# First queries and keys in two loads of 288 tokens, first scores in two steps, other offsets in the opening stretch

## The chip, the cores and the metric

One core of one Trainium2 chip. The metric is the device time of one execution in microseconds (us). The kernel before took 434.92 us, the median of 3 runs (434.41 to 435.18). Its program orders every instruction when it is built; nothing of the order is decided on the chip.

## The reference

Three stages, for 4 batches of 576 tokens, all in float32.

Stage 1 is attention with 8 heads of 64 values. Heads 0 to 3 look at the last 32 tokens (local), heads 4 to 7 at every 32nd token back (strided):

```python
mask_local = (rel >= 0) & (rel < stride)
mask_strided = (rel >= 0) & (pos[None, :] % stride == pos[:, None] % stride)
...
scores = np.where(masks[None, :, :, :], scores, -1000000000.0)
...
attn = attn / (np.sum(attn, axis=-1, keepdims=True) + 1e-09)
return np.matmul(attn, v).astype(np.float32)
```

Stage 2 is a gated block: `relu(x @ w_in)` is halved into u and v, v is normalised over its 512 features, mixed over the tokens with `w_spatial`, multiplied by u and projected by `w_out`. Stage 3 is four causal attention experts of width 64, of which each token takes the best two.

## The kernel before, in words

Every stage is written as small generators of steps. A step names its engine (or a choice of engines), a cost, what it needs and which buffers it takes. `Plan.run` (line 413 in the file, in class `Plan` from line 343) plays the steps through on a model of the five engines and emits them in that order: of the steps that can start first on an engine, the one with the lowest rank goes. The rank is given where a step is added (lines 1641 to 1724) plus an offset from the table NUDGE; HOLD delays a step's first start, and LEAN tilts the choice of engine. So three tables of numbers set the order of the work, on SP's queue of transfers too.

Attention works on pairs of heads: batch b, pair hp (0 and 1 local, 2 and 3 strided). `a1_load` (line 788) loads 64 + 64 rows of queries (line 796) and of keys (line 799), each a tile of 128 partitions by 576 tokens, 288 KB. `a1_load_v` (line 806) loads the values (line 818). `a1_scores` (line 826) does the small score matmuls (local: 36 blocks of 32 queries by 64 keys in two passes each, line 844; strided: line 856) in one step, into two PSUM tiles, one for each group of query blocks. `a1_local` (line 860) and `a1_strided` (line 916) mask a group on VectorE (lines 870 and 932), take the exponential on ScalarE (lines 879, 899) and scale by the sums, mostly on GpSimd (line 914). `a1_turn` transposes the weights on TensorE (lines 981, 983), and `a1_values` multiplies with the values (line 1050) and splits the result into a high and a low part, xh and xl (xl on VectorE, line 1062).

`weight` (line 652) loads a block of 128 rows of a weight (`w_in`: 512 KB of float64 bits, line 666, three buffers) and unpacks it, mostly on VectorE (lines 673 to 689 for the first half of the columns, the blocks W00 to W03; lines 673 to 698 and three matmuls at lines 705 to 707 for the second half, W10 to W13). Dense products are three matmuls for each pair of blocks (lines 618 to 620). `v_half` needs x of batch 0 and W10 to W13, block by block; `u_half` needs W00 to W03 as well. Until 46 us on its model, the planner fills TensorE's gaps with matmuls on zeros (`fill`, line 531), which compute nothing.

The ranks at the start: `a1_load` of batch 0 has 1.6 hp, `a1_load_v` 1.6 hp + 2.2, W1k 0.1 + 1.6 k, W0k 5 + k, and the attention of batch 1 has 100 + hp; to each comes its offset.

Of the kernel before, what the change touches and what calls it, by code (L numbers as in the profile page):

```python
# [1783 lines left out]
```

## Time and profile before

| what | value |
|---|---|
| median of 3 runs | 434.92 us (434.41 to 435.18) |
| the profiled execution | 434.02 us, of which the span of the profile is 432.1 us |
| TensorE, VectorE, ScalarE, GpSimd busy | 419.5, 318.7, 267.1, 141.1 us |
| data moved | 43.58 MB, mean 101 GB/s |
| granted TensorE clock | 0.998 over the span |

The profile shows one execution. The span runs from the first instruction to the last; 1.9 us lie around it. Busy times of different engines overlap. A row of the timeline gives start, busy time, engine, line, operation, tiles, count and, in brackets, how long the engine had been idle and for whom.

### The profile page before, as it was taken

To read this page: it belongs to the slowest core of one execution; us is meant where nothing else is said; L and a number is where in the kernel's file an instruction comes from. 1 tells how busy PE (TensorE), PEld (TensorE's weight loads), DVE (VectorE), ACT (ScalarE), POOL (GpSimd) and SP (SyncE) were. 2 spreads that over 40 slices of the span, in tenths; PEclk is the share of its full clock that TensorE was granted. 3 is DMA by queue.
4 is the path that set the end of the run, shared out by engine and by line. 5 is a ranking of instruction groups with operands and counts; after the bars stand their busy time and mean duration, and the time that the engine had idled before them with its cause. 6 is when DMAs were issued, how large, how long until landed. Compare 5 with 4: busy or idle time off the path is not lost.

```text
span 432.1 us, 11509 instructions
## 1 busy us (share of the span) xinstructions
PE 419.5 (97%) x4156; PEld 382.7 (89%) x4156; DVE 318.7 (74%) x1189; ACT 267.1 (62%) x827; POOL 141.1 (33%) x258
## 2 busy tenths in 40 slices
PE   7869999999999999999999999999999999999996
PEld 3557899999999889998999899999999999988885
DVE  6998998264577742347979863698888899988872
ACT  3666776154598841224405532887788779779973
POOL 3551876541152340221508911112022005215210
PEclk9999999999999999999999999999999999999999
DMA  7999105121561000334000006805251332162043
GB/s 297 340 361 308 35 2 175 67 79 36 157 205 44 2 2 2 122 101 167 2 1 2 2 0 155 194 1 126 67 134 43 94 79 58 24 160 98 26 148 121
DMA packets 22844, 43.58 MB, mean 101 GB/s; under 512 B 3202, under 2 KB 5634, under 8 KB 22788
## 3 DMA queue, kind: packets, MB, share of 16 engines
q1 hardware_dynamic: 22628, 42.72, 32.9%
q8 instruction: 33, 0.54, 0.5%
q14 instruction: 23, 0.19, 0.1%
q10 hardware_dynamic: 160, 0.13, 0.1%
HBM read 26.59 MB, written 4.72 MB: 72 GB/s over the span
## 4 chain that ended last, share of the span: by engine, by line
PE 95%; DVE 1%; DMA 1%; issue 1%; ACT 1%; POOL 0%; SPq 0%; ACTq 0%
PE pd L618 17%; PE pd L620 17%; PE pd L619 17%; PE pt L1488 4%; PE pd L1206 4%; PE pd L1207 4%; PE pd L1208 4%; PE px L1050 4%; PE ps L856 2%; PE px L1536 2%; PE ps L1401 2%; PE ps L1400 2%; PE px L1534 2%; PE px L1566 2%; PE pt L981 2%; PE pd L1210 1%
## 5 line engine op out<-in xcount | busy, mean ns | idle before, releaser
L1423 POOL TENSOR_SCALAR a<-a,asums 128x256 f32<-128x256 f32 (+3 forms) x23 | 23.1, 1010 | 87.1 <-DVE asums L1431 52.5
L914 POOL TENSOR_TENSOR a<-a,rs 128x216 f32<-128x216 f32 (+5 forms) x32 | 25.3, 797 | 55.2 <-DVE rs L912 26.3
L618 PE MATMUL pd<-xh,wh 128*128 128x288 f32 x128 | 38.8, 303 | 0.0
L1388 DVE CUSTOM_DVE_ANT_0 a<-ps,mqk 128x512 f32<-128x512 f32 (+4 forms) x72 | 33.5, 482 | 7.2 <-PE ps L1401 5.3
L1414 ACT ACTIVATE a<-a,amx 128x384 f32<-128x384 f32 (+3 forms) x64 | 35.6, 557 | 5.0 <-DVE amx L1388 4.9
L1206 PE MATMUL pd<-wh,vh 128*128 128x288 f32 x128 | 38.2, 298 | 0.0
L618 PE MATMUL pd<-gh,fh 128*128 128x288 f32 x128 | 38.1, 297 | 0.0
L619 PE MATMUL pd<-xl,wh 128*128 128x288 f32 x128 | 37.7, 295 | 0.0
L620 PE MATMUL pd<-gh,fl 128*128 128x288 f32 x128 | 37.7, 295 | 0.0
L1207 PE MATMUL pd<-wl,vh 128*128 128x288 f32 x128 | 37.7, 294 | 0.0
L620 PE MATMUL pd<-xh,wl 128*128 128x288 f32 x128 | 37.7, 294 | 0.0
L619 PE MATMUL pd<-gl,fh 128*128 128x288 f32 x128 | 37.7, 294 | 0.0
L1208 PE MATMUL pd<-wh,vlo 128*128 128x288 f32 x128 | 37.7, 294 | 0.0
L1121 DVE BATCH_NORM_STATS2 bst<-vr 128x6 f32<-128x512 f32 x18 | 12.4, 691 | 25.2 <-ACT vr L645 25.2
L1477 DVE TENSOR_TENSOR e<-pt,e 128x384 fp32r<-128x384 f32 (+1 forms) x48 | 27.6, 598 | 3.7 <-ACT e L639 3.2
L645 ACT ACTIVATE vr<-pd 128x512 f32<-128x512 f32 x17 | 10.1, 594 | 30.5 <-PE pd L620 29.0
L1214 DVE TENSOR_TENSOR u<-pd,u 128x288 f32<-128x288 f32 x32 | 13.9, 454 | 18.7 <-PE pd L1211 18.6
L1127 POOL TENSOR_TENSOR rstd<-rstd,neghalf 128x1 f32<-128x1 f32 x18 | 11.9, 664 | 47.4 <-DVE rstd L1125 38.7
L879 ACT ACTIVATE a<-a,mx 128x64 f32<-128x64 f32 (+1 forms) x72 | 24.9, 350 | 3.5 <-DVE mx L870 3.5
L618 PE MATMUL pd<-wh,xh 128*128 128x512 f32 x64 | 26.0, 406 | 0.0
L620 PE MATMUL pd<-wh,xl 128*128 128x512 f32 x64 | 25.1, 392 | 0.0
L619 PE MATMUL pd<-wl,xh 128*128 128x512 f32 x64 | 25.1, 392 | 0.0
(243 smaller groups left out, 1478.3 us busy)
## 6 DMA issues: line engine op xcount, KB each, us to landing
qk<-qk SPq DMA_DIRECT2D x64, 144.0 KB, 2.4
q<-in_qk_dram SPq DMA_DIRECT2D x16, 288.0 KB, 5.2
k<-in_qk_dram SPq DMA_DIRECT2D x16, 288.0 KB, 5.3
w<-in_win_dram SPq DMA_DIRECT2D x8, 512.0 KB, 6.3
out_dram<-o SPq DMA_DIRECT2D x16, 256.0 KB, 2.1
v<-in_vl_dram SPq DMA_DIRECT2D x8, 256.0 KB, 5.9
v<-in_vs_dram SPq DMA_DIRECT2D x8, 256.0 KB, 4.4
w<-in_woutT_dram SPq DMA_DIRECT2D x4, 512.0 KB, 4.4
```

The lines of the kernel that those rows point to most:

```text
L618: pe.matmul(ps, ah, bh, start=i == 0, stop=False)
L619: pe.matmul(ps, ah, bl, start=False, stop=False)
L620: pe.matmul(ps, al, bh, start=False, stop=i == n - 1)
L879: act.activation(a[:, c], a[:, c], AF.Exp, bias=mx[:, c:c + 1], scale=-1.0, accum_out=sums[:, c, :1])
L914: engine().tensor_mul(x, x, rs[:, :n].unsqueeze(2).broadcast_to([128, n, nk]))
L1206: pe.matmul(ps, vh[:, fs], wh[:, c0:c0 + cn], start=(i == 0), stop=False)
L1207: pe.matmul(ps, vh[:, fs], wl[:, c0:c0 + cn], start=False, stop=False)
L1208: pe.matmul(ps, vlo[:, fs], wh[:, c0:c0 + cn], start=False, stop=False)
L1388: dve.tensor_tensor_reduce(a[:, s0:s0 + sn], ps, mask, op0=ALU.add, op1=ALU.min, scale=-0.125, scalar=m if s0 else 3.0e38, accum_out=m)
L1414: act.activation(a, a, AF.Exp, bias=m, scale=-1.0, accum_out=st["sums", e][:, i:i + 1])
L1423: engine().tensor_scalar_mul(a, a, r)
L1477: dve.tensor_sub(el, ps, f(eh))
```

## The change

`a1_load` of the first pair of batch 0 loads queries and keys together, 288 tokens at a time, in two transfers; all other pairs load as before. `a1_scores` of that pair becomes two steps, one for each group, the first of which needs only the first transfer; a block of scores whose keys lie on both sides of token 288 becomes two matmuls. The event that the masks wait for is now one for each group. And the three tables are changed for the opening: the attention of batches 0 to 2, the `w_in` and spatial weights, and the first blocks of the dense products. The code, and of the tables the lines that set the first loads:

```diff
@@ NUDGE
-    'a1_load 0 0': -5.25, 'a1_load 0 1': -1.96, 'a1_load 0 2': 1.29, 'a1_load 0 3': 1, 'a1_load 1 0': 23.44,
...
+    'a1_load 0 0': -1.11, 'a1_load 0 2': 1.3, 'a1_load 0 3': 58.8, 'a1_load 1 0': -381.96, 'a1_load 1 1': 1.22,
+    'a1_load 1 2': -2.35, 'a1_load 1 3': -69.44, 'a1_load 2 0': 25.77, 'a1_load 2 1': -135.56, 'a1_load 2 2': 2.11,
+    'a1_load 3 1': 80.57, 'a1_load 3 2': 28.5, 'a1_load 3 3': 78.2, 'a1_load_v 0 0': 6.27, 'a1_load_v 0 1': 8.2,
+    'a1_load_v 0 2': 71.35, 'a1_load_v 0 3': 69.82, 'a1_load_v 1 0': 2.52, 'a1_load_v 1 1': -2.32,
...
-    'values 1 0': -15.65, 'values 1 1': -15.65, 'values 1 2': -15.61, 'values 1 3': -15.65, 'values 2 0': 0.85,
-    'values 2 1': -0.49, 'values 2 4': -8.96, "weight [('in', 0, 0)]": -10.61, "weight [('in', 0, 1)]": -0.46,
-    "weight [('in', 0, 2)]": -3.43, "weight [('in', 0, 3)]": -0.42, "weight [('in', 1, 0)]": -0.75,
-    "weight [('in', 1, 1)]": 1.68, "weight [('in', 1, 3)]": 0.53, "weight [('outT', 0)]": -4.4,
...
+    'values 1 3': -15.65, 'values 2 0': 0.85, 'values 2 1': -0.49, 'values 2 4': -8.96, "weight [('in', 0, 0)]": 0.06,
+    "weight [('in', 0, 2)]": -4.14, "weight [('in', 0, 3)]": -0.44, "weight [('in', 1, 1)]": 2.61,
+    "weight [('in', 1, 2)]": 0.1, "weight [('in', 1, 3)]": -0.23, "weight [('outT', 0)]": -4.4,
...
@@ HOLD
-    'a1_load 0 1': 2.27, 'a1_load 0 3': 0.02, 'a1_load 1 0': 0.9, 'a1_load 1 3': 1.52, 'a1_load 2 0': 20.87,
...
+    'a1_load 1 0': 0.5, 'a1_load 1 1': 0.03, 'a1_load 1 3': 3.52, 'a1_load 2 0': 20.03, 'a1_load 2 1': 7.79,
...
+    'values 3 0': 8.99, "weight [('in', 0, 0)]": 6.38, "weight [('in', 0, 2)]": 0.16, "weight [('in', 0, 3)]": 1.87,
+    "weight [('in', 1, 1)]": 2.04, "weight [('in', 1, 3)]": 7.88, "weight [('outT', 1)]": 0.58,
...
@@ a1_load
-        qt, kt = C([128, S], F, "q"), C([128, S], F, "k")
-        nc.sync.dma_start(qt, qk[b, hp, :, 0, :])
...
+        if n:
+            qt, kt = C([128, S], F, "q"), C([128, S], F, "k")
...
+        else:
+            qt, kt = [], []
+            for i, (c0, cn) in enumerate(HALVES):
+                if i:
+                    yield "sp", 0.46, (), {}
+                t = C([128, 2, cn], F, "qk1")
+                nc.sync.dma_start(t, qk[b, hp, :, :, c0:c0 + cn])
+                plan.dma(128 * 2 * cn * 4)
+                plan.set(("qk", b, hp, i), plan.ready - plan.end)
+                qt.append(t[:, 0])
+                kt.append(t[:, 1])
...
@@ a1_scores
-        yield "pe", (0.8 if large else 1.15 if local else 0.95), [("qk", b, hp)], dict(s=2)
...
+        def product(out, r, q0, qn, k0, kn):
+            if type(qt) is not list:
+                pe.matmul(out, qt[r, q0:q0 + qn], kt[r, k0:k0 + kn], start=True, stop=True)
+                return
+            q = qt[q0 // 288][r, q0 % 288:q0 % 288 + qn]
+            cut = min(max(288 - k0, 0), kn)
+            for c0, c1 in ((0, cut), (cut, kn)):
+                if c0 < c1:
+                    i = (k0 + c0) // 288
+                    pe.matmul(out[:, c0:c1], q, kt[i][r, k0 + c0 - 288 * i:k0 + c1 - 288 * i], start=True, stop=True)
+
+        whole_pair = b or hp
+        cost = 0.8 if large else 1.15 if local else 0.95
+        for groups in ((0, 1),) if whole_pair else ((0,), (1,)):
+            yield ("pe", cost if whole_pair else cost / 2, [("qk", b, hp) if whole_pair else ("qk", b, hp, groups[0])],
+                   dict(s=len(groups)))
...
+            if groups == (0,):
+                plan.set(("s1", b, hp, 0))
...
@@ a1_local
-        yield "dve", t_dve(n * nk, n), [("mask", "wide" if wide(b, hp) else True), ("s1", b, hp)], dict(c=1, mx=1)
+        yield "dve", t_dve(n * nk, n), [("mask", "wide" if wide(b, hp) else True), ("s1", b, hp, g)], dict(c=1, mx=1)
```

## Rows read from the trace of the kernel before

**Rows 1.** The page: busy time of each engine, and the chain by engine

```profile
PE 419.5 (97%) x4156; PEld 382.7 (89%) x4156; DVE 318.7 (74%) x1189; ACT 267.1 (62%) x827; POOL 141.1 (33%) x258
...
PE 95%; DVE 1%; DMA 1%; issue 1%; ACT 1%; POOL 0%; SPq 0%; ACTq 0%
```

**Rows 2.** Busy time by stretch: length, engines, then clock, DMA share, GB/s

```profile
0.00:5.04 5.04, 3.59 (x8) 1.04 (x8) 1.32 (x7) 1.49 (x2) 3.61 (x29) 1.00 0.54 169
5.04:37.33 32.29, 25.20 (x598) 17.99 (x598) 29.76 (x139) 17.86 (x68) 11.64 (x28) 1.00 0.98 353
37.33:60.00 22.67, 22.67 (x333) 19.17 (x333) 21.44 (x116) 19.56 (x73) 16.92 (x29) 1.00 0.32 98
60.00:400.00 340.00, 339.97 (x3047) 320.15 (x3047) 246.27 (x870) 205.07 (x629) 105.46 (x168) 1.00 0.28 76
400.00:432.10 32.10, 28.10 (x174) 24.39 (x172) 19.89 (x60) 23.10 (x56) 3.43 (x5) 0.97 0.28 99
```

**Rows 3.** The same for line 531 alone, 0 to 37.33 us: the sum

```profile
sum 37.33, PE 9.08 PEld 2.89; mean PE 4.54 PEld 1.44
```

**Rows 4.** Timeline of TensorE around the first dense matmuls and the last wait

```profile
30.52 0.49 PE L618 MATMUL pd<-wh,xh 128*128 128x512 f32 x1
...
37.00 0.33 PE L1050 MATMUL px<-aT,v 36*64 36x36 f32 x7 [0.72 <-issue]
37.26 0.50 PE L618 MATMUL pd<-wh,xh 128*128 128x512 f32 x1
```

**Rows 5.** Waits of TensorE: us in total, times, longest

```profile
PE px L1050 <- issue: 2.6, 2, 1.9
PE ps L844 <- DMA k<-in_qk_dram: 2.0, 1, 2.0
PE pt L981 <- POOL a L914: 1.5, 2, 1.2
PE pt L981 <- issue: 1.4, 1, 1.4
```

**Rows 6.** Timeline of all engines, 0 to 12 us

```profile
0.80 0.39 SPq L666 DMA_DIRECT2D w<-in_win_dram  x1
...
1.25 0.42 SPq L796 DMA_DIRECT2D q<-in_qk_dram  x1
...
1.71 0.43 SPq L799 DMA_DIRECT2D k<-in_qk_dram  x1
...
5.04 0.43 DVE L673 TENSOR_SCALAR a<-w 128x512 int32<-128x512 int32 x1 [2.16 <-DMA w<-in_win_dram]
...
6.61 2.15 PE L844 MATMUL ps<-k,q 64*32 64x64 f32 x72 [1.97 <-DMA k<-in_qk_dram]
...
7.83 0.69 DVE L689 SCALAR_TENSOR_TENSOR wl<-a,p 128x512 fp32r<-128x512 f32 x1
...
8.82 0.23 DVE L870 CUSTOM_DVE_ANT_0 a<-ps,mloc 128x64 f32<-128x64 f32 x1 [0.29 <-PE ps L844]
...
11.72 1.21 PE L844 MATMUL ps<-k,q 64*32 64x64 f32 x72
```

**Rows 7.** Issue to landing of line 799's loads, then of tile w's

```profile
DMA to landing us min/median/max: 2.8/5.3/7.7
...
DMA to landing us min/median/max: 4.2/6.3/7.1
```

**Rows 8.** Timeline of all engines, 10 to 18 us

```profile
10.06 0.33 SPq L799 DMA_DIRECT2D k<-in_qk_dram  x1
...
12.19 0.99 POOL L914 TENSOR_TENSOR a<-a,rs 128x320 f32<-128x320 f32 x1 [7.69 <-ACT a L879]
...
17.42 0.74 SPq L796 DMA_DIRECT2D q<-in_qk_dram  x1
...
17.49 0.20 DVE L932 CUSTOM_DVE_ANT_0 a<-ps,mstr 128x54 f32<-128x54 f32 x1
```

**Rows 9.** Waits of VectorE, 2 to 45 us

```profile
DVE xl L1062 <- ACT xh L639: 1.7, 2, 1.2
```

More of the change, by code (lines that the diff above doesn't have):

```diff
@@ L107 @@
     'g_split 2 3': 51.57, 'g_split 3 2': 33.33, 'g_split 3 3': -131.8, 'g_tail 0': -7.49, 'g_tail 1': -3,
[1 row of a table removed]
-    "opens ('proj', 0)": 33.35, "opens ('proj', 1)": 34.4, "opens ('proj', 2)": -7.26, "opens ('proj', 3)": 6.61,
[27 rows of a table removed]
-    "weight [('in', 1, 1)]": 1.68, "weight [('in', 1, 3)]": 0.53, "weight [('outT', 0)]": -4.4,
[1 row of a table added]
+    "opens ('proj', 1)": 34.4, "opens ('proj', 2)": -7.26, "opens ('proj', 3)": 6.61, 'opens late weights': 59.21,
[26 rows of a table added]
+    "weight [('in', 1, 2)]": 0.1, "weight [('in', 1, 3)]": -0.23, "weight [('outT', 0)]": -4.4,
     "weight [('outT', 1)]": 90.83, "weight [('outT', 2)]": 0.22, "weight [('outT', 3)]": 165.35,
@@ L314 @@
-    ('v_tail 0', 8, 'dve'): -1.4, ('values 1 2', 1, 'act'): -3, ('values 2 4', 1, 'act'): 1,
-    ("weight [('in', 0, 0)]", 0, 'dve'): 1, ("weight [('in', 0, 0)]", 1, 'act'): 3,
-    ("weight [('in', 0, 0)]", 2, 'pool'): 1, ("weight [('in', 0, 1)]", 3, 'dve'): -0.6,
+    ('late_constants', 1, 'act'): 6, ('late_constants', 2, 'pool'): 3, ('late_constants', 3, 'dve'): 1,
+    ('late_constants', 6, 'act'): 3, ('late_constants', 6, 'dve'): 0.4, ("opens ('a1', 2)", 0, 'dve'): 2.6,
[14 rows of a table added]
+    ('spatial_tail', 1, 'dve'): 9, ('spatial_tail', 1, 'pool'): 2, ('spatial_tail', 2, 'act'): 0.6,
@@ new lines @@
+    ('spatial_tail', 3, 'dve'): 0.4, ('spatial_tail', 5, 'act'): -1, ('spatial_tail', 5, 'dve'): 1,
+    ('spatial_tail', 5, 'pool'): 3, ('spatial_tail', 6, 'dve'): 6.4, ('spatial_tail', 6, 'pool'): -0.4,
+    ('spatial_tail', 7, 'dve'): -0.4, ('spatial_tail', 7, 'pool'): 1, ('u_half 0 0 0', 0, 'act'): -3,
[35 rows of a table added]
+    ('v_half 3 3', 0, 'act'): -3, ('v_tail 0', 8, 'dve'): -1.4, ('values 1 2', 1, 'act'): -3,
+    ('values 2 4', 1, 'act'): 1, ("weight [('in', 0, 0)]", 0, 'dve'): -0.4, ("weight [('in', 0, 0)]", 0, 'pool'): 0.4,
@@ L317 @@
+    ("weight [('in', 0, 0)]", 1, 'act'): 3, ("weight [('in', 0, 0)]", 2, 'pool'): 1,
+    ("weight [('in', 0, 0)]", 3, 'act'): 3, ("weight [('in', 0, 0)]", 3, 'dve'): 3,
+    ("weight [('in', 0, 1)]", 0, 'dve'): -0.4, ("weight [('in', 0, 1)]", 3, 'act'): 1.6,
     ("weight [('in', 0, 2)]", 1, 'act'): 4, ("weight [('in', 0, 2)]", 1, 'dve'): 4,
     ("weight [('in', 0, 2)]", 3, 'dve'): -0.4, ("weight [('in', 0, 2)]", 3, 'pool'): -1,
-    ("weight [('in', 0, 3)]", 1, 'act'): 1, ("weight [('in', 0, 3)]", 2, 'act'): -5.8,
@@ L320 @@
-    ("weight [('in', 0, 3)]", 2, 'dve'): -3, ("weight [('in', 1, 0)]", 2, 'dve'): -0.4,
-    ("weight [('in', 1, 0)]", 2, 'pool'): 0.4, ("weight [('in', 1, 0)]", 4, 'pool'): 1,
-    ("weight [('in', 1, 1)]", 3, 'act'): -3.4, ("weight [('in', 1, 1)]", 3, 'dve'): -1,
-    ("weight [('in', 1, 2)]", 0, 'dve'): 3, ("weight [('in', 1, 2)]", 0, 'pool'): -1,
-    ("weight [('in', 1, 3)]", 0, 'dve'): 0.4, ("weight [('in', 1, 3)]", 0, 'pool'): -3,
-    ("weight [('in', 1, 3)]", 2, 'dve'): 3, ("weight [('in', 1, 3)]", 2, 'pool'): 7,
@@ L326 @@
-    ("weight [('in', 1, 3)]", 4, 'dve'): -3, ("weight [('in', 1, 3)]", 5, 'act'): -3,
-    ("weight [('outT', 1)]", 2, 'dve'): 0.4, ("weight [('outT', 3)]", 0, 'act'): -0.4,
-    ("weight [('outT', 3)]", 0, 'dve'): 1, ("weight [('pqk', 0)]", 1, 'act'): 3,
-    ("weight [('pqk', 1)]", 0, 'act'): -1, ("weight [('pvg', 2), ('pvg', 3)]", 0, 'act'): -6,
-    ("weight [('sp', 0)]", 0, 'act'): 6.4, ("weight [('sp', 0)]", 0, 'dve'): 8.6,
-    ("weight [('sp', 0)]", 0, 'pool'): -1, ("weight [('sp', 0)]", 1, 'act'): -3, ("weight [('sp', 0)]", 2, 'act'): 1,
@@ L338 @@
-    ('x_tail 1 0', 0, 'dve'): -2, ('x_tail 1 0', 0, 'pool'): 5, ('x_tail 1 1', 0, 'act'): -0.4,
-    ('x_tail 1 1', 0, 'dve'): 0.4, ('x_tail 2 2', 0, 'dve'): -1, ('x_tail 3 0', 0, 'dve'): -3,
-    ('x_tail 3 1', 0, 'act'): 1,
+    ("weight [('in', 0, 3)]", 1, 'dve'): -0.4, ("weight [('in', 0, 3)]", 2, 'act'): -0.4,
+    ("weight [('in', 0, 3)]", 2, 'dve'): 1, ("weight [('in', 0, 3)]", 3, 'dve'): 1,
+    ("weight [('in', 1, 0)]", 4, 'pool'): 1, ("weight [('in', 1, 0)]", 5, 'dve'): 5.6,
+    ("weight [('in', 1, 0)]", 5, 'pool'): -0.4, ("weight [('in', 1, 1)]", 2, 'pool'): -2.6,
@@ new lines @@
+    ("weight [('in', 1, 1)]", 3, 'act'): -3, ("weight [('in', 1, 2)]", 0, 'dve'): 3,
+    ("weight [('in', 1, 2)]", 0, 'pool'): -1, ("weight [('in', 1, 2)]", 4, 'dve'): 0.4,
+    ("weight [('in', 1, 2)]", 4, 'pool'): -2, ("weight [('in', 1, 3)]", 0, 'dve'): -3.6,
+    ("weight [('in', 1, 3)]", 0, 'pool'): -3, ("weight [('in', 1, 3)]", 2, 'pool'): 6,
+    ("weight [('in', 1, 3)]", 4, 'dve'): -3, ("weight [('in', 1, 3)]", 4, 'pool'): -3.4,
+    ("weight [('in', 1, 3)]", 5, 'act'): -3, ("weight [('outT', 1)]", 2, 'dve'): 0.4,
@@ new lines @@
+    ("weight [('outT', 3)]", 0, 'act'): -0.4, ("weight [('outT', 3)]", 0, 'dve'): 1,
+    ("weight [('pqk', 0)]", 1, 'act'): 3, ("weight [('pqk', 1)]", 0, 'act'): -1,
+    ("weight [('pvg', 2), ('pvg', 3)]", 0, 'act'): -6, ("weight [('sp', 0)]", 0, 'act'): 3,
+    ("weight [('sp', 0)]", 0, 'dve'): 3, ("weight [('sp', 0)]", 0, 'pool'): -1, ("weight [('sp', 0)]", 1, 'act'): -3,
+    ("weight [('sp', 0)]", 2, 'act'): 1, ("weight [('sp', 0)]", 2, 'dve'): -0.4, ("weight [('sp', 1)]", 1, 'pool'): 1,
@@ new lines @@
+    ("weight [('sp', 1)]", 2, 'pool'): -3, ("weight [('sp', 2)]", 0, 'act'): -3,
+    ("weight [('sp', 2)]", 0, 'dve'): 0.6, ("weight [('sp', 2)]", 0, 'pool'): -2,
+    ("weight [('sp', 2)]", 1, 'dve'): -1, ("weight [('sp', 2)]", 1, 'pool'): 0.4, ("weight [('sp', 2)]", 2, 'act'): 1,
+    ("weight [('sp', 2)]", 2, 'pool'): 0.4, ("weight [('sp', 3)]", 0, 'act'): 5.2,
+    ("weight [('sp', 3)]", 0, 'dve'): 7.4, ("weight [('sp', 3)]", 0, 'pool'): -2,
+    ("weight [('sp', 3)]", 2, 'act'): -0.6, ("weight [('sp', 3)]", 2, 'dve'): -0.2,
@@ L341 @@
+    ("weight [('wo', 1)]", 0, 'act'): 1, ("weight [('wo', 1)]", 0, 'dve'): 1, ('x_tail 0 0', 0, 'act'): -1,
[3 rows of a table added]
 }
@@ L794, in a1_load @@
         yield "sp", 0.46, [("a1", b)] + prev, dict(c=2)
-        qt, kt = C([128, S], F, "q"), C([128, S], F, "k")
-        nc.sync.dma_start(qt, qk[b, hp, :, 0, :])
-        plan.dma(128 * S * 4)
-        yield "sp", 0.46, (), {}
-        nc.sync.dma_start(kt, qk[b, hp, :, 1, :])
-        plan.dma(128 * S * 4)
+        A1[b, hp] = dict(nk=64 if local else 54, v=[], a={}, x=None, ps=[None] * 2)
+        if n:
+            qt, kt = C([128, S], F, "q"), C([128, S], F, "k")
+            nc.sync.dma_start(qt, qk[b, hp, :, 0, :])
+            plan.dma(128 * S * 4)
+            yield "sp", 0.46, (), {}
+            nc.sync.dma_start(kt, qk[b, hp, :, 1, :])
+            plan.dma(128 * S * 4)
+        else:
+            qt, kt = [], []
+            for i, (c0, cn) in enumerate(HALVES):
+                if i:
+                    yield "sp", 0.46, (), {}
+                t = C([128, 2, cn], F, "qk1")
[4 more added lines that the diff above has]
+                kt.append(t[:, 1])
+        A1[b, hp].update(q=qt, k=kt)
         r = plan.ready
         plan.set(("ld", b, hp))
-        A1[b, hp] = dict(q=qt, k=kt, nk=64 if local else 54, v=[], a={}, x=None)
         plan.set(("qk", b, hp), r - plan.end)
@@ L832, in a1_scores @@
         large = wide(b, hp)
-        yield "pe", (0.8 if large else 1.15 if local else 0.95), [("qk", b, hp)], dict(s=2)
-        st = A1[b, hp]
-        nk, qt, kt = 96 if large else st["nk"], st["q"], st["k"]
-        st["ps"] = [P([128, n[g], nk], "s") for g in range(2)]
-        if local and not large:
-            for g, (c0, c1) in enumerate(LOCAL_GROUPS):
+        def product(out, r, q0, qn, k0, kn):
[13 more added lines that the diff above has]
+                   dict(s=len(groups)))
+            st = A1[b, hp]
+            nk, qt, kt = 96 if large else st["nk"], st["q"], st["k"]
+            for g in groups:
+                st["ps"][g] = P([128, n[g], nk], "s")
+            for g in groups if local and not large else ():
+                c0, c1 = LOCAL_GROUPS[g]
                 for c in range(c0, c1):
@@ L842, in a1_scores @@
                             j, r, p = 2 * c + s, slice(64 * h, 64 * h + 64), 64 * h + 32 * s
-                            k0 = max(32 * j - 32, 0)
-                            pe.matmul(st["ps"][g][p:p + 32, c - c0, :], qt[r, 32 * j:32 * j + 32], kt[r, k0:k0 + 64],
-                                      start=True, stop=True)
+                            product(st["ps"][g][p:p + 32, c - c0, :], r, 32 * j, 32, max(32 * j - 32, 0), 64)
+            if groups == (0,):
+                plan.set(("s1", b, hp, 0))
         for c in range(0 if local and not large else max(n)):
@@ L855, in a1_scores @@
                     r, o = slice(64 * h, 64 * h + 64), slice(64 * (h ^ g), 64 * (h ^ g) + 64)
-                    pe.matmul(st["ps"][g][o, c, :w], qt[r, q0:q0 + 64], kt[r, k0:k0 + w], start=True, stop=True)
+                    product(st["ps"][g][o, c, :w], r, q0, 64, k0, w)
         plan.give("c", 2)
-        plan.set(("s1", b, hp))
+        for g in range(2) if whole_pair else (1,):
+            plan.set(("s1", b, hp, g))
     def a1_local(b, hp, g):
@@ L925, in a1_strided @@
             pool.memset(a[:, 7, :54], 0.0)
-        yield "dve", t_dve(n * 54, n), [("mask", False), ("s1", b, hp)], dict(mx=1)
+        yield "dve", t_dve(n * 54, n), [("mask", False), ("s1", b, hp, g)], dict(mx=1)
         st = A1[b, hp]
```

26 lines of the change are left out of this document (9 added, 17 removed), and 369 rows, old and new, of tables (HOLD, LEAN, NUDGE).

## The prediction

> **What bounds the kernel now.** I read the page's busy table and its chain first: TensorE is busy for 97% of the span, and 95% of the chain that ended last is TensorE [rows 1]. So time can only be won where TensorE has no useful matmul. The table of stretches says where that is: from 37.33 to 60 us TensorE is busy for all of the 22.67 us, from 60 to 400 us for 339.97 of 340 us; what it leaves idle at the very end (4.0 us of the last 32.1) is not touched by the change [rows 2]. Up to 37.33 us it is busy for 3.59 + 25.20 = 28.79 us, and 9.08 us of that are matmuls on zeros (line 531), which only fill time [rows 2, 3]. So 19.7 us of the first 37.33 are useful, and 17.6 us are not: that is the most the opening can give back, and the change can win nowhere else.
>
> What keeps TensorE waiting there is not TensorE. In the 32.29 us from 5.04 to 37.33, VectorE is busy for 29.76 us, and the DMA engines have a share of 0.98 at 353 GB/s [rows 2]. The reader should see two full resources feeding a third: data arrive at the ceiling, VectorE unpacks weights and does the softmax of batch 0, and TensorE gets what comes out. The last wait of the opening ends at 37.00 us (0.72 us before the values step of line 1050), dense matmuls run from 37.26 us on, and the first of them ran at 30.52 us [rows 4]. Four waits of TensorE stand out: 2.6 us in two pieces before line 1050, 2.0 us for the first keys, 1.5 us for GpSimd's scaled weights, 1.4 us before line 981 [rows 5].
>
> The start in detail [rows 6]: SP issues a 512 KB weight (W00 below: "in", 0, 0) at 0.80 us, the first queries at 1.25 and the keys at 1.71. VectorE begins to unpack W00 at 5.04 and is at it until 7.83 + 0.69 = 8.52 us. The first scores wait for the keys until 6.61 and take 2.15 us for 72 matmuls (the same 72 of the next pair of heads take 1.21 us). Though they are done at 8.76, and the mask of the first local step starts at 8.82, VectorE could hardly have taken them sooner: it was unpacking. So what is late first is data, and what is late next is VectorE.
>
> **The change, part by part.** *Order of the first loads.* By the ranks (line 1646 and 1657, plus the offsets) the first load of SP is now that of the queries and keys (-1.11), then W10 (0.1), the second pair of heads (1.6), W02 (2.86), W12 (3.4); W00 falls from -5.61 to 5.06, with a hold of 6.38. Each half load has 128 x 2 x 288 x 4 bytes = 288 KB, as each of the two old ones, so there are two issues as before (0.42 and 0.43 us of SP) [rows 6]. The first half then has nothing ahead of it. When it lands is not in the trace: the bounds are 0.80 + 2.8 = 3.6 us, the shortest landing of a load of keys, and 0.80 + 4.2 = 5.0 us, the shortest of the 512 KB weight [rows 6, 7]. I take 4.0, nearer the row of its own size. The fixed part dominates: the Trainium skill, page "DMA: Bandwidth & Descriptors", section "Anatomy of one DMA", gives about 2.0 us plus bytes over 436 GB/s (fitted on GpSimd's path); for 512 KB that makes 3.2 us where the row has 4.2 at the least, so the rule is too fast here, and by it the half would land at 3.5 us and the sum below be 0.25 us better.
>
> *Rows of half the length.* A partition's run falls from 2304 to 1152 bytes. No row of this trace prices that; it costs nothing if the rate holds, and at worst the two halves run as slowly as the stretch before 5.04 us, 169 GB/s [rows 2], where 288 KB take 1.7 us in place of 0.84 at 353 GB/s: 0 to 0.9 us on the second half alone. I take 0.
>
> *Scores in two steps.* Group 0 (16 of 36 blocks, 32 of 72 matmuls) needs only the first half. One block of 32 queries has its 64 keys on both sides of token 288: two heads, two passes, 4 more matmuls at 2.15/72 = 0.03 us, 0.1 us, beside a TensorE that waits anyway. Group 0 takes 32/72 of 2.15 = 0.96 us [rows 6], from 4.0 to 5.0, and the mask of group 0 can start at about 5.1 us where the first one started at 8.82: a head start of 3.7 us for the first pair of heads, 3.2 to 4.2 with the other bounds. GpSimd's scaling of the weights (12.19), with ScalarE's exponentials between them, can follow it: GpSimd has stood idle for 7.69 us by then [rows 8].
>
> *What VectorE does with it.* Its work is moved, not removed. It started at 5.04 us and starts at about 5.1. The 3.48 us of W00 no longer stand ahead of the first mask; but W02, an equal unpacking, still comes before the second pair's masks, and W10 lands only as third transfer, about where the keys did (6.6), so between the two masks there can be a gap. Of the 3.7 us, between nothing (the same total of VectorE's work ends at the same time) and all (one unpacking goes behind the point from which TensorE is full) reaches TensorE. With VectorE at 29.76 of 32.29 neither end can be excluded, and I take the middle: **1.85 us**.
>
> *The other offsets.* Some hundreds of entries of the three tables change, for attention of batches 0 and 1, the "in" and spatial weights and the first dense block. I cost them at nothing on the sum: TensorE's work is the same, and after 37.33 us it hides what VectorE, ScalarE and GpSimd do (from 60 to 400 us VectorE, the fullest of them, is busy for 246 of 340) [rows 2]. If that cover went, VectorE would be first: it is busy for 21.44 of 22.67 us from 37.33 to 60. One entry is large and moves transfers: the loads of batch 1's first heads go from rank 123 to -282, held only until 0.5 us after the first pair's weights are done; see the third rival. Another moves the fourth pair of batch 0 from 5.8 to 63.6, behind the values.
>
> **The sum.** The profiled execution took 434.02 us (span 432.1 and 1.9 around it), 0.90 below the median of 434.92. Minus 1.85: 432.2 in its terms, **433.1** against the median. A difference of about 0.2%, 0.9 us, is what a measurement of this kernel can tell from none.
>
> **The rivals.**
>
> *The whole head start, and VectorE's own waits too* (0.17). If the unpacking goes wholly behind and the new offsets also close VectorE's two waits for ScalarE's xh (1.7 us) [rows 9], the gain is 3.7 + 1.7 = 5.4: 429.5 us. For it: 17.6 us are there to be won, and TensorE's waits at lines 1050 and 981 are all waits for this chain [rows 5]. Against it: VectorE is already full.
>
> *Hidden anyway* (0.15). The DMA engines have 0.98 of their time taken and VectorE 0.92 of it up to 37.33 us; what is first in a full queue only changes who waits. Then 434.9, within 0.9. The Trainium skill, the same page, section "Specifications", puts a core's HBM limit at about 358 GB/s; the trace agrees with 353 GB/s [rows 2], and by that rule an order of loads moves no more bytes by 37 us. Against it: the loads up to there include those of batch 1 and weights that are not needed first, so the order can matter.
>
> *Slower: batch 1's early loads* (0.20). Its queries and keys, 576 KB, were issued at 17.42 us, after all of batch 0's [rows 8]; by the new rank they go as soon as the first pair is done, ahead of the queries and keys of batch 0's fourth pair (63.6), of its values (76.8) and of the last weights. In a full queue that is 0.59 MB over 353 GB/s = 1.7 us for whatever stands behind, and the fourth pair's chain is what TensorE waits for last (line 1050, 37.00 us) [rows 4]. If that chain then starts later than VectorE would have come to it, the opening ends 1.7 us later and not sooner: 434.9 + 1.7 = 436.6. It decides from the point where the fourth pair's keys land after the third pair's masks are done; the issue at 10.06 with 5.3 us to land (median) and the first strided masks only at 17.49 leave some 2 us of room, which is why it has no more than 0.20 [rows 7, 8].
>
> That the change doesn't do what it says is not a case: the loads and the scores are in the code, and need no luck.
>
> **How the numbers follow.** The forecast has 0.48, with a range of its own from 431.2 (all of the 3.7) to 434.0. Faster by more than 0.2%: that 0.48 and the 0.17 of the first rival: 0.65. Same: 0.15. Slower: 0.20. The range of 8 in 10 takes in the forecast's, most of the first rival and most of the third: 430.0 to 436.2.
>
> **What would show it.** Right: the first scores start at about 4.0 and their mask at about 5.1 us; W00 is unpacked later than 8.5 us; zero-matmuls below 9.1 us; the stretch from which TensorE has no wait begins 1 to 3.7 us before 37.33, and the tail keeps its length. Wrong: a first half that lands at 5 us or later; a VectorE with a new gap of over 1 us between 5 and 8 us; a new wait of TensorE past 37 us, for W13, for the spatial weights or for batch 1; or fourth-pair masks later than before.

## The result and the profile after

The changed kernel takes 437.31 us (median of 11 runs, 435.84 to 438.85), the kernel before 434.52 us beside it (11 runs, 433.32 to 436.00). The ratio is 1.0054, 95% interval 1.0034 to 1.0075: **slower by 1.5 to 3.3 us**, where the forecast was 1.85 us faster and the range ended at 436.2. The profiled execution took 437.42 us, span 435.6.

Busy times and the chain of the page after, the lines that answer to [rows 1]:

```profile
PE 424.5 (97%) x4165; PEld 383.8 (88%) x4165; DVE 323.9 (74%) x1196; ACT 264.8 (61%) x817; POOL 144.8 (33%) x261
...
PE 87%; DVE 8%; DMA 1%; POOL 1%; issue 1%; ACT 1%; SPq 1%; POOLq 0%; DVEq 0%
```

VectorE's share of the chain is 8%, where it was 1%: followed back from its end, the chain now runs over VectorE for some 35 us. The same stretches as [rows 2], after:

```profile
0.00:5.04 5.04, 2.64 (x33) 1.19 (x37) 1.31 (x6) 1.49 (x2) 3.63 (x29) 1.00 0.48 141
5.04:37.33 32.29, 29.15 (x551) 19.08 (x542) 26.68 (x134) 18.66 (x68) 11.70 (x25) 0.95 0.99 347
37.33:60.00 22.67, 22.02 (x364) 17.41 (x364) 21.24 (x117) 17.33 (x67) 17.25 (x27) 1.00 0.35 113
60.00:400.00 340.00, 339.59 (x3042) 319.28 (x3041) 252.40 (x875) 202.19 (x622) 106.28 (x175) 1.00 0.27 75
```

In the second row VectorE has lost 3.08 us of busy time (26.68 for 29.76), and TensorE's granted clock is 0.95 where it was 1.00: its 29.15 us of busy time are partly slower matmuls, not more of them. The opening of the changed kernel, timeline of 0 to 9 us:

```profile
0.80 1.35 SPq L843 DMA_DIRECT2D qk<-in_qk_dram  x2
...
2.19 0.60 SPq L700 DMA_DIRECT2D w<-in_win_dram  x1
...
4.29 1.17 PE L890 MATMUL ps<-qk 64*32 64x64 f32 x34 [1.35 <-DMA qk<-in_qk_dram]
...
5.43 0.23 DVE L935 CUSTOM_DVE_ANT_0 a<-ps,mloc 128x64 f32<-128x64 f32 x1 [2.55 <-PE ps L890]
...
6.50 0.23 DVE L935 CUSTOM_DVE_ANT_0 a<-ps,mloc 128x64 f32<-128x64 f32 x1 [0.40 <-PE ps L890]
...
8.46 0.43 DVE L707 TENSOR_SCALAR a<-w 128x512 int32<-128x512 int32 x1 [1.15 <-DMA w<-in_win_dram]
```

The change does what it says: the first scores run at 4.29 us and the first mask at 5.43, 3.39 us ahead of the 8.82 of [rows 6]. But VectorE waits between the two groups (0.40 us, for the second half's scores) and behind them (1.15 us) for the first weight, W10, which lands at 8.4; in the kernel before W00 had landed by 5.04 [rows 6]. Windows of 5 us (length; PE, PEld, DVE, ACT, POOL; clock, DMA share, GB/s), first of the kernel before, then of the changed one:

```profile
0.00:5.00 5.00, 3.59 (x8) 1.04 (x8) 1.31 (x6) 1.49 (x2) 3.61 (x29) 1.00 0.53 168
5.00:10.00 5.00, 3.39 (x76) 2.42 (x77) 4.42 (x17) 1.48 (x6) 0.00 (x0) 1.00 1.03 409
...
20.00:25.00 5.00, 3.08 (x114) 2.72 (x110) 4.86 (x33) 3.68 (x10) 2.74 (x5) 1.00 1.01 384
5.00:60.00 55.00, 47.87 (x930) 37.16 (x930) 51.20 (x255) 37.42 (x141) 28.56 (x57) 1.00 0.71 248
```

```profile
0.00:5.00 5.00, 2.60 (x32) 1.15 (x36) 1.31 (x6) 1.49 (x2) 3.63 (x29) 1.00 0.48 141
5.00:10.00 5.00, 4.57 (x71) 2.15 (x62) 2.95 (x22) 3.45 (x19) 0.00 (x0) 1.00 0.92 293
...
20.00:25.00 5.00, 5.00 (x55) 3.40 (x56) 3.21 (x38) 2.49 (x8) 2.81 (x9) 0.66 0.97 351
5.00:60.00 55.00, 51.21 (x917) 36.53 (x908) 47.92 (x250) 36.00 (x135) 28.95 (x52) 0.97 0.73 250
```

Three things are to be read here. From 5 to 10 us VectorE loses 1.47 us (2.95 for 4.42). From 20 to 25 us it loses 1.65 us more (3.21 for 4.86), at a granted clock of 0.66. Up to 60 us it is short by 3.28 us (47.92 for 51.20), and TensorE's last matmul begins 2.97 us later (430.79 for 427.82). Transfers are behind too: times 5 us, the first two rows make 0.84 + 2.05 = 2.88 MB by 10 us before and 0.70 + 1.47 = 2.17 MB after.

How the second loss comes about, one microsecond at a time, in the changed kernel:

```profile
18.00:19.00 1.00, 0.00 (x0) 0.00 (x0) 0.96 (x4) 0.20 (x1) 0.06 (x1) 1.00 1.05 353
19.00:20.00 1.00, 0.11 (x1) 0.11 (x2) 0.97 (x5) 0.00 (x0) 1.00 (x2) 1.00 1.00 351
20.00:21.00 1.00, 1.00 (x5) 0.70 (x5) 1.00 (x16) 0.38 (x1) 0.88 (x2) 0.77 1.06 373
21.00:22.00 1.00, 1.00 (x3) 0.41 (x2) 1.00 (x10) 0.38 (x1) 0.57 (x2) 0.50 0.94 362
22.00:23.00 1.00, 1.00 (x5) 0.54 (x3) 0.44 (x3) 0.00 (x0) 0.75 (x5) 0.50 1.06 393
23.00:24.00 1.00, 1.00 (x33) 0.88 (x34) 0.00 (x0) 0.77 (x3) 0.55 (x1) 0.52 0.99 344
```

TensorE is idle from 17.8 to 19.9 us; then its granted clock is 0.50 (1.2 GHz, half of 2.4) for about 3.4 us, up to about 24, its matmuls take longer, and VectorE is without work from 22.5 us on. The timeline has what led to the wait and one of the slower matmuls. The waits of VectorE (us in total, times, longest) follow: the first is what the slow stretch cost it, the second the earlier one for W10.

```profile
17.82 0.69 DVE L723 SCALAR_TENSOR_TENSOR wl<-a,p 128x512 fp32r<-128x512 f32 x1
...
18.43 0.15 DVE L974 TENSOR_REDUCE rs<-eps 128x4 f32<-128x8 f32 x1
...
18.94 1.58 POOL L979 TENSOR_TENSOR a<-a,rs 128x256 f32<-128x256 f32 x2 [2.98 <-DVE rs L977]
...
19.89 0.44 PE L1046 MATMUL pt<-ident,a 128*128 128x128 f32 x2 [2.12 <-POOL a L979]
...
20.17 1.53 PE L739 MATMUL px<-a,ident 128*128 128x512 f32 x2
```

```profile
DVE a L997 <- PE ps L883: 1.7, 1, 1.7
DVE a L707 <- DMA w<-in_win_dram: 1.1, 1, 1.1
```

TensorE waits for GpSimd, but GpSimd itself had stood idle for 2.98 us, for VectorE's row sums. The last of that group's exponentials began at 15.76 us and they ended at about 16.2; VectorE was then in the second half of W02's unpacking, whose last step begins at 17.82, and took the sums only behind it, at 18.43. So the wait is one for VectorE, and for the order of its steps.

### The profile page after: what moved, and what is told of

The parts are those of the page before. It is cut to its first block, busy times and chain, and to the rows that moved or that the text cites. A ratio compares the mean times of both kernels' runs of the same rounds, so it can differ in the third digit from the quotient of the medians.

```text
span 435.6 us, 11528 instructions
## 1 busy us (share of the span) xinstructions
PE 424.5 (97%) x4165; PEld 383.8 (88%) x4165; DVE 323.9 (74%) x1196; ACT 264.8 (61%) x817; POOL 144.8 (33%) x261
## 4 chain that ended last, share of the span: by engine, by line
PE 87%; DVE 8%; DMA 1%; POOL 1%; issue 1%; ACT 1%; SPq 1%; POOLq 0%; DVEq 0%
PE pd L652 16%; PE pd L653 15%; PE pd L654 15%; PE pt L1553 4%; PE pd L1271 4%; PE pd L1273 4%; PE pd L1272 4%; PE px L1115 3%; PE ps L883 3%; PE px L1601 2%; PE ps L1466 2%; PE ps L1465 2%; PE px L1599 2%; PE px L1631 2%; DMA k<-in_qk_dram 1%; PE pt L1046 1%
## 5 line engine op out<-in xcount | busy, mean ns | idle before, releaser
L979 POOL TENSOR_TENSOR a<-a,rs 128x216 f32<-128x216 f32 (+5 forms) x30 | 23.2, 783 | 39.6 <-DVE rs L977 24.7
L1174 POOL TENSOR_TENSOR vlo<-vr,vh 128x512 fp32r<-128x512 f32 x14 | 19.1, 1368 | 20.8 <-ACT vh L673 10.4
L673 ACT ACTIVATE aT<-pt 128x256 f32<-128x256 f32 (+5 forms) x35 | 14.6, 442 | 18.5 <-PE pt L1025 9.5
L679 ACT ACTIVATE vr<-pd 128x512 f32<-128x512 f32 x15 | 9.0, 597 | 26.7 <-PE pd L654 25.1
```

The source lines that it names most:

```text
L979: engine().tensor_mul(x, x, rs[:, :n].unsqueeze(2).broadcast_to([128, n, nk]))
```

## The experiments

Theory 1: VectorE paces the kernel up to about 60 us, and what it lacks by then TensorE's last matmul is late. Rival 2: only the half clock costs. Rival 3: batch 1's early loads. Rival 4 (later): the transfers and the chain of scores and exponentials are the pace, and VectorE only follows. Where a text says that the order is held, the planner's loop was replaced by its own record: the list of steps in the order in which it took them, with engine and number of zero matmuls. The list is that of the kernel named there, but for the steps shown as moved.

**The code alone.** The split loads and scores, with the three tables of the kernel before.

```diff
-NUDGE, HOLD, LEAN: as changed
+NUDGE, HOLD, LEAN: as before
```

> The change's code (first queries and keys in two loads of 288 tokens, first scores in two steps) with the three tables of the kernel before: the first weight stays ahead of the first loads, and VectorE starts on that weight. Theory 1 (the change loses because VectorE, which paces the opening, runs dry behind the first masks until a weight lands): here it has the first weight's 3.4 us of work as before, so nothing is lost, ratio to before 0.998 to 1.002. Rival (the loads of half length and the second scores step cost the time themselves): ratio 1.003 or more. Rival (batch 1's early loads, which only the tables bring): ratio 0.998 to 1.002 as well.

435.41 us (12 runs), ratio 1.0038, interval 1.0011 to 1.0064: slower, outside theory 1's numbers and inside those of the rival that the split itself costs. The timeline shows why VectorE stood still for all that:

```profile
7.95 0.27 PE L856 MATMUL ps<-qk,qk 64*32 64x32 f32 x2 [1.16 <-DMA qk<-in_qk_dram]
...
9.27 0.22 DVE L901 CUSTOM_DVE_ANT_0 a<-ps,mloc 128x64 f32<-128x64 f32 x1 [1.03 <-PE ps L856]
```

Here the tables take the second group first; its half landed at 7.9 us, so VectorE was dry for 1.03 us behind W00. A second loss follows at 28 to 34 us, in the same shape as in the changed kernel (a TensorE idle for 2.65 us, then a granted clock of 0.66 from 30 to 35 us).

**The tables alone**, on the code of before.

```diff
-NUDGE, HOLD, LEAN: as before
+NUDGE, HOLD, LEAN: as changed
```

> The kernel before with the changed kernel's three tables and whole first loads: queries and keys go out first, the first weight behind them, batch 1's first loads early. Theory 1: VectorE has no weight to start on, its first mask waits for both whole tiles (about 5.5 to 6 us) and then for the weight; it ends some 1.5 to 3 us behind before, ratio 1.003 to 1.008. Rival (the split itself costs): ratio 0.998 to 1.002.

456.31 us (6 runs), ratio 1.0516, interval 1.0487 to 1.0545. The sign is theory 1's, the size is not: these offsets are made for the timing of the split, and on the other code they give another order throughout. Of use is its opening: with whole loads ahead of W10, the weight landed at 8.31 us too.

```profile
8.31 0.43 DVE L707 TENSOR_SCALAR a<-w 128x512 int32<-128x512 int32 x1 [0.46 <-DMA w<-in_win_dram]
```

**The short rows alone**, in the order of before.

```diff
-nc.sync.dma_start(qt, qk[b, hp, :, 0, :])
+nc.sync.dma_start(qt.rearrange("p (a c) -> p a c", a=2), qk[b, hp, :, :, :288])
...
-nc.sync.dma_start(kt, qk[b, hp, :, 1, :])
+nc.sync.dma_start(kt.rearrange("p (a c) -> p a c", a=2), qk[b, hp, :, :, 288:])
```

> The kernel before, order and tables as they are, with its first queries and keys fetched as two halves of 288 tokens instead of as whole queries and whole keys; the scores still wait for both. It tells what the short rows alone cost, behind the first weight. Forecast's term (rows of half length cost nothing to 0.9 us of landing, hidden behind the first weight): ratio 0.999 to 1.001. Rival (as in the run with the code alone, the second load lands some 1.3 us later, at 7.9 for 6.6 us, and VectorE's first mask at 9.3 for 8.8): 0.5 us or more late, ratio 1.001 to 1.004.

434.69 us (12 runs), ratio 1.0011, interval 0.9991 to 1.0031: no difference shown. The first mask started at 8.50 us, no later than before. By 10 us 2.70 MB had been moved, 0.18 less. Its profile has two stretches of half clock that the profile of the kernel before has not (0.72 from 5 to 10 us, 0.50 from 25 to 30), so nothing is read from how late that one profile ends.

**VectorE given 2 us more**, early and late. Three reductions of 512 columns into a scratch tile, ahead of the first masks, or ahead of the masks of one group at 96 us.

```diff
+if (b, hp, g) == (0, 0, 1):
+    for _ in range(3):
+        dve.tensor_reduce(scratch, ident.unsqueeze(1).broadcast_to([128, 4, 128]), op=ALU.add, axis=AX.X)
```

> The kernel before with three idle reductions of 512 columns (about 1.9 us in all, 0.65 us each by the reductions of 216 and 378 columns) on VectorE ahead of the first masks at 8.8 us; every engine's order is otherwise that of before. Theory 1 (VectorE paces the opening until about 60 us, so what it loses there the end loses): the time grows by 1.3 to 1.9 us, ratio 1.003 to 1.0045. Rival 2 (only TensorE's half-clock stretch at 20.5 to 24 us costs): under 0.4 us, ratio under 1.001.

> The same three reductions on VectorE ahead of the masks of one late group (about 96 us), where VectorE is busy 11.2 of 20 us and TensorE all of it. Theory 1: VectorE does not pace there, so the time stays, ratio 0.999 to 1.0012. Rival (any microsecond of VectorE's costs one): ratio 1.003 to 1.0045.

Early: 436.07 us (7 runs), ratio 1.0051, interval 1.0032 to 1.0070. Late: 434.35 us (12 runs), 1.0019, 0.9999 to 1.0038. The early reductions took 2.12 us and pushed the first mask to 10.41:

```profile
8.26 2.12 DVE L867 TENSOR_REDUCE scratch<-ident 128x4 f32<-128x512 f32 x3
10.41 0.23 DVE L873 CUSTOM_DVE_ANT_0 a<-ps,mloc 128x64 f32<-128x64 f32 x1
```

Early they cost about their full length, 2.2 us by the ratio, more than the expected 1.3 to 1.9. Late TensorE's last matmul of the profile begins 0.2 us later (428.04); the ratio is above the expected 1.0012, and the times leave up to 0.4% open. So time put on VectorE in the opening is paid for at the end. But the early run's profile has half clock in two stretches as well (0.69 from 15 to 20 us, 0.68 from 30 to 35) and its last matmul 2.87 us later (430.69): how much of the price is VectorE's own time, and how much the half clock behind the waits that it made, is not separated.

**TensorE's gap filled.** The order held; before the transposes at 19.89 us the list's count of zero matmuls goes from 0 to 5.

```diff
-a1_turn 0 1 0, step 0: TensorE, 0 zero matmuls
+a1_turn 0 1 0, step 0: TensorE, 5 zero matmuls
```

> The changed kernel, its order of all steps held, with five more zero matmuls (some 0.35 us each by their mean, 1.75 us in all) on TensorE where it waited 2.12 us at 17.8 us, so that it is not idle ahead of the stretch that was granted half clock. Rival 2 (the half clock costs VectorE its 1.7 us of wait, and so the end): the granted clock stays at 1.0 from 20 to 24 us, the scores of the third pair come 1 to 1.5 us earlier, ratio 1.002 to 1.003. Theory 1 alone (only the 1.5 us at 5 to 10 us count): ratio 1.0045 to 1.006.

436.13 us (12 runs), ratio 1.0049, interval 1.0029 to 1.0069. In the profile the clock stayed at 1.00 and VectorE got its 1.57 us back (4.78 for 3.21):

```profile
20.00:25.00 5.00, 5.00 (x98) 3.57 (x98) 4.78 (x50) 2.88 (x9) 3.91 (x10) 1.00 1.01 364
5.00:60.00 55.00, 52.10 (x925) 37.45 (x917) 49.52 (x252) 37.73 (x141) 30.42 (x54) 1.00 0.72 250
```

TensorE's last matmul begins 1.60 us earlier (429.19). That is about half of the loss in the profiled execution. In the median it is less, some 1.2 us (437.37 in the run below, on the same chip), the intervals of the two overlap, and the ratio lies in the numbers given for theory 1 alone.

**Batch 1's loads late again.**

```diff
-'a1_load 1 0': -381.96
+'a1_load 1 0': 23.44, with its HOLD of 0.9
```

> The changed kernel with the offset and hold of batch 1's first queries and keys as in the kernel before, so that they go out later again; the order of TensorE's instructions stays. Rival 3 (their early transfer takes bandwidth from the weights and tokens that the opening waits for): 1 us or more is given back, ratio 1.003 or less. Theory 1 (the loss is made before 10 us, when they aren't out yet): no change, ratio 1.0045 to 1.0065.

437.37 us (7 runs), ratio 1.0074, interval 1.0045 to 1.0102. But the edit moved nothing: the planner's list of steps is the same with it as in the changed kernel. Batch 1's first loads wait for the first pair's weights, and by then those of batch 0's fourth pair have gone out (13.50 and 14.26 us). Timeline of SP, batch 1's first queries in the changed kernel:

```profile
17.05 0.33 SPq L832 DMA_DIRECT2D q<-in_qk_dram  x1
```

In this run they went out at 17.17 us. So it is one more series of the changed kernel and no test of rival 3. What speaks against the rival is the row above: in the kernel before the same load went out at 17.42 us [rows 8], so the changed kernel brought it forward by 0.37 us only, and not ahead of batch 0's.

**A weight first, to fill VectorE's dry spell.** The order held, but for the moved steps.

```diff
+SP: load W10
 SP: first half, second half
-SP: load W10
...
+VectorE: unpack W10, first step
 VectorE: masks of group 0, of group 1
-VectorE: unpack W10, first step
```

> The changed kernel with its order of all steps held as it is, but for two: the first weight's load goes out ahead of the two halves, and VectorE unpacks it ahead of the first masks. Theory 1 (VectorE ran dry for 0.4 and 1.15 us because the weight landed at 8.46): the weight lands near 5 us as the first weight did before, VectorE starts there, the halves land at about 6 and 8, so its steps run on with at most about 1 us of wait (as in the run with the code alone); the end comes 1 to 2.5 us ahead of the changed kernel's, ratio to before 1.000 to 1.003. Rival (VectorE's dry spell is not the cause): ratio 1.0045 or more, as the changed kernel (1.0054).

437.10 us (6 runs), ratio 1.0067, interval 1.0041 to 1.0093: a miss. And with W00, which changes places with W02:

```diff
+SP: load W00
 SP: first half, second half
...
+VectorE: unpack W00, first step
 VectorE: masks of group 0
+VectorE: unpack W00, second step
 VectorE: masks of group 1
```

> The changed kernel, its split loads and its order of all steps held, but for one weight: the weight of the gates' first chunk changes places with that of its third chunk, goes out ahead of the two halves as in the kernel before, and VectorE unpacks it in two steps (some 1.5 and 1.9 us) ahead of the first and of the second masks. Theory 1 (VectorE paces the opening; what the change lost is the time it stood dry between 5 and 8.5 us and what followed from that): VectorE starts near 5 us and does not run dry before 15 us; its busy time from 5 to 60 us is 50.5 us or more, and the end comes 2 to 4 us ahead of the changed kernel's, ratio to before 0.996 to 1.001. Rival (the loss sits in the split itself or in the later order): ratio 1.003 or more.

> The same with the five zero matmuls ahead of the transposes of the second pair's first group, as in the run that filled the gap. Theory 1: if TensorE's wait there is gone, they cost nothing, since VectorE paces (ratio within 0.001 of the run without them); if a wait of 2 us is left and half clock follows it, they give back up to 1.6 us as they did there. Rival: they cost their 1.75 us, ratio 0.004 above the run without them.

> The changed kernel as it is, beside the two above on the same chip, as the measure for them and for the runs that edit it. Every theory: ratio 1.0035 to 1.0075, as in its own comparison.

W00 first: 437.90 us (6 runs), 1.0076, 1.0057 to 1.0096. With the zero matmuls as well: 438.65 (6 runs), 1.0096, 1.0074 to 1.0119. The changed kernel beside them: 437.42 (6 runs), 1.0067, 1.0042 to 1.0092. Misses again, and the profiles point to why: the dry spell only moves. W10 first leaves VectorE idle until the halves have landed behind it; W00 first is busy there, and stands still at 16 us instead, where it has no second weight left and the second pair's exponentials are late. Timeline of VectorE, of the first and then of the second:

```profile
8.13 0.23 DVE L935 CUSTOM_DVE_ANT_0 a<-ps,mloc 128x64 f32<-128x64 f32 x1 [1.71 <-PE ps L890]
```

```profile
18.17 0.16 DVE L974 TENSOR_REDUCE rs<-eps 128x4 f32<-128x8 f32 x1 [2.02 <-ACT a L944]
```

**VectorE work taken away** from the kernel before, its order held.

```diff
-cast of W10's low part: VectorE
+cast of W10's low part: ScalarE
-a1_strided 0 2 1 and 0 3 0, subtraction of the maxima: VectorE
+a1_strided 0 2 1 and 0 3 0, subtraction of the maxima: GpSimd
```

> The kernel before with the order of all steps held and three of VectorE's steps of the opening given to other engines: the cast of the second weight's low part (0.68 us at 16.9) to ScalarE, two subtractions of the row maxima (0.56 us at 19.5, 0.87 us at 23.2) to GpSimd; 2.1 us of VectorE's work in all. Theory 1 (VectorE paces to 60 us): the end comes 1 to 2.1 us earlier, ratio 0.995 to 0.998. Rival 4 (the opening is paced by transfers and by the chain of scores, exponentials and transposes, VectorE only follows): the same work on slower engines makes the chain longer, ratio 0.999 to 1.003.

> The kernel before with only the cast of the second weight's low part (0.68 us at 16.9) moved from VectorE to ScalarE, which is idle a quarter of that stretch; its result is wanted only by the products near 30 us. Theory 1: 0.3 to 0.7 us earlier, ratio 0.998 to 0.9995. Rival 4: no change, 0.9995 to 1.001.

All three: 434.71 us (12 runs), 1.0015, 0.9988 to 1.0042. The cast alone: 434.00 (12 runs), 0.9993, 0.9969 to 1.0018. No gain is shown, as rival 4 said. The waits of VectorE in the first of the two, 5 to 45 us:

```profile
DVE xl L1062 <- ACT xh L639: 1.8, 2, 1.0
DVE eps L902 <- ACT a L899: 1.0, 2, 0.8
```

The time freed turns into waits for ScalarE; before it had 1.7 us of the first [rows 9] and none of the second. So theory 1 is borne out one way only: time put on VectorE is paid for at the end, time taken off it is not won. The work was moved to ScalarE and GpSimd, though, and not removed, so what VectorE's time alone would give stays open.

**Whole loads in the changed order.** The order held, the two halves replaced by whole queries and whole keys, alone and with TensorE's gap filled.

```diff
-nc.sync.dma_start(t, qk[b, hp, :, :, c0:c0 + cn])
+nc.sync.dma_start(t.rearrange("p a c -> p (a c)"), qk[b, hp, :, i, :])
```

> The changed kernel with the order of all steps held, but its two first loads are whole queries and whole keys (2304-byte rows) in the place of the two halves (1152 bytes); both groups' scores then wait for the keys. If the short rows make the shortfall: by 10 us 2.5 MB or more are moved (2.17 in the changed kernel), the first weight lands 0.5 us or more earlier, VectorE's busy time from 5 to 60 us rises by 0.5 to 1.5 us, and the end comes as much earlier: ratio 1.002 to 1.005. If the order makes it (the weight behind the first pair): the weight lands past 8 us all the same, as with the tables alone (8.31), the first masks start past 6 us in place of 5.4, and nothing is won: ratio 1.0055 to 1.008.

> The same with the five zero matmuls in TensorE's gap ahead of the second pair's transposes. If the half clock's price (1.6 us in the profile of the run that filled the gap) is there in this order too: 0.7 to 1.6 us ahead of the run with whole loads. If the gap is gone with whole loads: level with it.

437.31 us (12 runs), ratio 1.0042, interval 1.0019 to 1.0066; filled, 435.22 (12 runs), 1.0015, 0.9999 to 1.0032. 2.45 MB were moved by 10 us in both, for 2.17. W10 landed by 7.79 us in one profile and at 8.52 in the other:

```profile
7.79 0.43 DVE L707 TENSOR_SCALAR a<-w 128x512 int32<-128x512 int32 x1
```

```profile
8.52 0.43 DVE L707 TENSOR_SCALAR a<-w 128x512 int32<-128x512 int32 x1 [0.91 <-DMA w<-in_win_dram]
```

Neither of the two cases expected of whole loads is met in full: more was moved by 10 us, but VectorE's busy time rose by 0.24 us only. So no worth of the split, either way, is shown in this order. The fill is the best that the changed order came to: the two medians are 2.1 us apart, more than the expected 0.7 to 1.6, and the intervals overlap only between 1.0019 and 1.0032. No version is shown to be faster than the kernel before.

**The runs in two numbers**, from the windows and the timelines of their profiles: VectorE's busy time from 5 to 60 us, and the start of TensorE's last matmul, each against the kernel before (51.20 us and 427.82), with TensorE's granted clock from 5 to 60 us (1.00 before):

| run | VectorE short by | last matmul late by | clock |
|---|---|---|---|
| changed kernel | 3.28 | 2.97 | 0.97 |
| the same again | 2.82 | 2.55 | 0.97 |
| the same, with batch 1's edit | 3.72 | 3.40 | 0.97 |
| gap filled | 1.68 | 1.37 | 1.00 |
| whole loads | 3.04 | 2.90 | 0.97 |
| whole loads, gap filled | 2.04 | 1.65 | 1.00 |
| W00 first | 2.66 | 2.07 | 1.00 |
| W00 first, gap filled | 2.98 | 2.10 | 1.00 |
| W10 first | 4.81 | 3.34 | 0.97 |
| code alone | 2.12 | 1.85 | 0.97 |
| half rows | 0.97 | 1.34 | 0.91 |
| early reductions, without their 2.12 | 1.96 | 2.87 | 0.94 |
| late reductions | -0.06 | 0.22 | 0.97 |
| three steps off VectorE | 1.09 | 0.39 | 0.97 |
| one step off VectorE | 2.07 | 1.64 | 0.94 |

The first six share one order, and there one number follows the other within 0.4 us. It is a measure of how far the preparation of batches 0 and 1 is behind, and no proof that VectorE is its cause: with three steps taken off VectorE (2.1 us) it was busy for 1.09 us less, and the last matmul came 0.39 us later. The W00 rows show that a loss of some 2 us is left where the clock stays at 1.00 and VectorE starts at 4.78 us.

## Why the prediction was wrong, step by step

- **The bound.** Right: all that changed lies in the opening, and past 60 us TensorE is as full as it was (339.59 of 340 us). That two full resources feed TensorE there was right as well, and was not drawn on enough: what one is short of, the other can't make good.
- **First half at 4.0 us, mask at 5.1.** Near: 4.2 by the 3.4 us from issue to landing, and 5.43. An estimate by the Trainium skill's formula ("DMA: Bandwidth & Descriptors", "Anatomy of one DMA") has the half at 3.5 us; the trace bears it out no better here than for the weight, and the measured 3.4 us from issue to landing decide.
- **Rows of half the length, 0 to 0.9 us, taken as 0.** Not refuted: 1.0011, with an interval that holds 1.
- **The step that failed: "what VectorE does with it", half of the head start, 1.85 us.** It put the lower end at nothing, because VectorE's work "is moved, not removed" and because it "started at 5.04 us and starts at about 5.1". That holds only while something has landed for it to do. In the kernel before, W00's 3.48 us of unpacking cover the time in which queries, keys and W10 arrive. With the halves first, 32 + 40 short score matmuls feed VectorE for under 2 us, and W10, which I had landing "about where the keys did (6.6)", came at 8.4, as the third transfer. The gap "between the two masks" was named and not priced: 0.40 us there and 1.15 behind. And W02, which was said to come "before the second pair's masks", came behind them and ahead of their sums, so what was moved away from the first masks stood in the second pair's way. So the sum needed an end below nothing, where it had +1.85: about 1.5 us from the dry spell, and in all 3.28 us of VectorE's time by 60 us, with TensorE's last matmul 2.97 us later.
- **What was not foreseen.** TensorE waits 2.12 us for GpSimd at 17.8 us, and GpSimd for VectorE's sums; half clock follows, and VectorE waits 1.7 us for the scores. Whether the late start or the order of VectorE's steps makes that wait is not separated. Filling the gap gave back 1.60 us of the 2.97 in the profile. What causes the other 1.37 is the dry opening by the windows; no run removed that spell without making another (with W00 first the last matmul was 2.07 us late, at full clock), so this half is argued from the trace and from the early reductions, not shown by taking it away.
- **Other offsets at nothing.** Put at nothing because TensorE's work is the same; not borne out, for the order of VectorE's steps that led to the wait at 17.8 us comes from them. Their price is not separated: the code alone is at 1.0038, code and tables at 1.0054, and the intervals overlap. New waits past 37 us are there, as the text said a wrong forecast would show (0.6 us for a weight's low part, line 654).
- **The rivals.** The slower one had the sign, by luck: its condition did not come about. Batch 1's first queries went out at 17.05 us, against 17.42 before, and behind the fourth pair's loads, not ahead of them; the rank was read without the wait for the first pair's weights. "Hidden anyway" came closest in its reason, that the full queue only changes who waits, and missed the loss. The new order did not move the same bytes, though, but fewer: 293 GB/s for 409 from 5 to 10 us. The limit of about 358 GB/s that the Trainium skill gives ("DMA: Bandwidth & Descriptors", "Specifications") fits the 353 of the whole opening, and not these five microseconds: 409 lies above it, so the limit says nothing on what an order is worth there.

## What to carry to other kernels

When a load is moved ahead, ask what the engine behind it did in the meantime: the work that seemed to stand in the way may be the cover under which the rest arrives, and the price of an earlier start then has an end below zero. Where two resources are both over 90% busy, expect an answer that differs by direction: here 2.12 us put on VectorE cost about 2.2, and 2.1 us moved off it gave nothing that could be measured. And after a wait of some 2 us on TensorE look at the granted clock of the next few microseconds before blaming the wait alone.
